# Turning q and probabilities with VectorE and a trip through DRAM, in the steady part of a fused attention and feed-forward kernel on one core

## The chip, the cores and the metric

The kernel runs on one core of a Trainium2 chip. The metric is the device time of one execution in microseconds. The core's engines run their own instruction streams: TensorE (PE) multiplies matrices, VectorE (DVE) and ScalarE (ACT) work on elements, GpSimd (POOL) does next to nothing here, and SyncE (SP) issues all transfers of the steady part in the order of its stream. Engines wait for each other and for transfers through semaphores.

## The reference

Attention over 8 batches, 8 heads, 576 tokens, 64 dimensions, with keys and values averaged in groups of eight tokens (72 pooled ones), followed by a feed-forward network with a softplus:

```
k_p = k.reshape(B, H, 72, 8, D).mean(axis=3);  v_p likewise
scores = (q @ k_p.T) / sqrt(D)
attn = exp(scores - max(scores));  attn /= sum(attn) + 1e-09
x = (attn @ v_p) as [4608 tokens, 512]
out = softplus(x @ w_in[512, 2048]) @ w_out[2048, 512]
```

All is float32. In this kernel the feed-forward products run as three products of rounded parts (a high and a low part of each factor).

## The kernel before, in words

The 4608 tokens are cut into 18 chunks of 256 (`CT`), each of two tiles of 128 tokens (`T`). The program has a first part, which splits the weights into high and low parts and works off chunks 0 to 2 with an order of its own, and a **steady part**, from chunk 3 on (`N1`), which the change is about. It begins at about 168 us of the span.

In the steady part a chunk's feed-forward work is eight **pairs** of weight blocks, u = 0 to 7. A pair has *first products* (`pair1`, 24 matmuls of 128x256 into a bank `h`, L727) and *second products* (from chunk 4, `NF`, on: `pair2_fast`, 21 matmuls into the banks `m`, L879, a scheme of seven products in place of eight). Between them stand ScalarE's two softplus passes (`g` L735, `gh` L749), VectorE's `gl` (L756), four additions `sf` (L789 to L792), and the split of the sums into `so` (ScalarE L803, VectorE L808). The first products of pair u are followed by the second products of pair u-1, so that these have a pair's time. The first-layer weights of a pair, two blocks of 512 KB, are streamed from DRAM by `load_wi` (L907) into one of two places; their issue waits for the first products two pairs ahead.

While chunk c is in its feed-forward part, the attention of chunk c+1 is done between its pairs (`steady_attention` and `probabilities`):

- q is loaded (`load_q_tile` L363, 128 tokens x 8 heads x 64), turned by eight 128x128 transposes on TensorE into two banks `qTp` (`Tile.qT`, L394), and copied out by ScalarE (`qT_out`, L401);
- the scores are made (`pair_scores`, L541), VectorE takes off the least and writes `E` (L563, L579), ScalarE makes the exponentials in place (L355, with a change of its function table);
- VectorE, once per tile, sums (L445), adds 1e-9 and inverts (L449, L450), multiplies into `pm` (keys 0 to 63, L454) and `pe` (keys 64 to 71, L589), and turns `pm` in blocks of 32x32 into `turn` (`turn`, L512). Four transfers within the core (`spread`, L518, 128 KB each) then bring the blocks to the partitions where they belong, in `pT`;
- the attention products (`av_products`, L641 and L648, tile `avp`) read `pT` and the pooled values and give the next chunk's `x` (L655, L658).

The order is written by a planner, the class `Order`: a list scheduler. Each piece of work (`op`) has an engine, a cost, what it comes after, the buffers it needs and a lag; its rank is the length of the chain behind it plus a number `first`, and the engines' streams are written in the order of the planned starts. Nothing of the plan is decided on the chip: each engine, SP's queue among them, works its own stream in order and waits where it must.

In both kernels the buffers are named by kinds with a few places each (`ld`, `G`, `qT`, `bank` and others); the pooled keys and values, which come through `ld`, are made in `keys_values`. Turned blocks are read back by `blocks` (L521).

```
before = first_products(c, u, before)
if u == EXP and c + 1 < NCH:
    rest(third[c, u])          # exponentials after this pair's sums
if u: before = second_products(c, u - 1, before)
```

Of the kernel before, what the change touches and what calls it, by code (L numbers as in the profile page):

```python
# [108 lines left out]
def pooled_attention_softplus_ffn(  # L109
# [14 lines left out]
    P = 128  # L124
# [381 lines left out]
    B32 = 32  # L506
    turned_ = set()
    A = P // B32
# [12 lines left out]
    def blocks(x, t):  # L521

        return x.rearrange("p a (i u m) -> p u m (a i)", u=T, m=HP)[:, t]
# [402 lines left out]
    def act(n):  # L926
        return 0.14 + 0.00094 * n
# [338 lines left out]

    def keys_values(b, free_k=None, free_v=None):
# [9 lines left out]
        def pooled(load, pool, time, slot, after=()):  # L1277

            s = Slot("ld")
            o = op(SYNC, time, lambda: load(s), ends[-2:][:1], [s], lag=2.4)  # L1280
            ends.append(op(DVE, 1.4, pool, [o, *after], [s, slot]))
            return ends[-1]

        sums_ = [pooled(lambda s, i=i: x["k_load"](i, s), lambda i=i: x["k_pool"](i), 1.2, s_kp)
                 for i in range(HP)]
        s_t = Slot("bank")
        o = op(PE, 0.3, lambda: k_transposes(bank(s_t, "kT"), x["kp"][0]), [*sums_, *free_k],
               [s_t, s_kp], first=100, home=None if todo.last else "h")
        k_ready[b] = [op(ACT, act(288), lambda: k_scaled(b, s_t.tile), [o], [s_t])]
        sums_ = [pooled(lambda s, i=i: x["v_load"](i, s), lambda i=i: x["v_pool"](i), 1.2, s_vp)  # L1290
                 for i in range(2)]
        v_ready[b] = [op(ACT, act(256), lambda: v_scaled(b, x["vp"][0]), [*sums_, *free_v], [s_vp])]
        o = pooled(lambda s: x["left_load"](s), x["left"], 1.0, s_vl, v_ready[b])
        o = op(DVE, 1.1, x["lasts"], [o, *k_ready[b]], [s_vl, s_lt])
        parts = [op(ACT, 0.65, lambda i=i: left_part(b, i, x["st"]["lt"]), [o, *free_v], [s_lt])
                 for i in range(2)]
        v_ready[b].append(op(DVE, 0.7, lambda: left_part(b, 2, x["st"]["lt"]), parts, [s_lt]))

    def combinations(u, free=None):
# [6 lines left out]
        for part in range(2):  # L1306
# [5 lines left out]
            if s:  # L1312
                o = op(SYNC, 2.0, lambda part=part: put_t(u, part), [o], s, lag=2.4,
                       first=0 if todo.last else 1000)
# [54 lines left out]
    op = todo.op  # L1369
    EXP, third = 2, {}  # L1370
    HURRY, EARLY = 60, 100
    MM = 0.1142
    TURN, SPREAD = 0.75, 3.0
# [6 lines left out]

    def steady_attention(c):
# [5 lines left out]
        o_q = op(SYNC, 3.0, load, qT_done.get(c - 1, ()), [s_q], lag=2.4)  # L1387
# [3 lines left out]
        s_qT, s_qb = [Slot("qT") for _ in tiles], [Slot("bank") for _ in tiles]  # L1391

        def transposes():
            for x, s in zip(tiles, s_qb):
                x.qT(bank(s, "qTp"))
        o = op(PE, 0.89, transposes, [o_q, *av_done.get(c - 1, ())], [s_q, *s_qb], first=EARLY, home="m")
        qT_done[c].append(o)
        for x, s, n in zip(tiles, s_qb, s_qT):
            x_q.append(op(ACT, act(512), lambda x=x, s=s, n=n: x.qT_out(s.tile, n.name), [o], [s, n]))
# [5 lines left out]
        p = op(PE, 1.4, lambda: pair_scores(  # L1405
# [3 lines left out]
        for j in (2, 0, 1):  # L1409
            ps = lambda j=j: third_bank() if j == 2 else ss[j].tile  # L1410
            o = op(DVE, 0.3 if j == 2 else 0.68,
                   lambda j=j, ps=ps: pair_least(c, j, ps(), s_mn.name), [p], [ss[j], s_mn],
                   first=HURRY if j == 2 else 0)
            for part in range(1 if j == 2 else 3):
                subs.append(op(DVE, 0.3 if j == 2 else (0.46, 0.3, 0.22)[part],
# [4 lines left out]
    def probabilities(c, tiles, s_E, s_lt, subs, where):  # L1420

        s_pT, lows, s_pe, es = Slot("pT"), [], Slot("pe"), []
        turns, turned, s_t = {}, [], Slot("ld")
        ex = op(ACT, 1.2 + TABLE, lambda: exponential(e_[c]), [*subs, where], [s_E])
        op(ACT, TABLE, lambda: None, [ex], first=5000)
        for x in tiles:
            s_sm, s_pm = Slot("sm"), Slot("G")
            o = op(DVE, 0.76, lambda x=x, n=s_sm: x.sum(n.name), [ex], [s_E, s_sm])
            o = op(DVE, 0.38, x.reciprocal, [o], [s_sm])
            m = op(DVE, 0.7, lambda x=x, s=s_pm: x.main(s.name), [o], [s_E, s_sm, s_pm])  # L1430
# [207 lines left out]
```

## Time and profile before

| | us |
|---|---|
| median of three runs | 871.7 (870.2, 871.7, 875.04) |
| the profiled execution | 874.31 |
| its span | 872.6 |
| mean granted TensorE clock | 0.999 |
| TensorE busy | 861.0, 8642 instructions |
| VectorE busy | 669.8, 1629 instructions |
| ScalarE busy | 405.3, 824 instructions |
| HBM read and written | 167.25 and 22.54 MB, 218 GB/s over the span |

The span is the time from the first to the last instruction on the core that the profile shows; the execution's own time is 1.7 us more. Busy time leaves out waiting. A matmul's record runs until its result is out and matmuls overlap, so the start of the next row tells what a group costs, not the sum of its records.

### The profile page before, as it was taken

The page shows a single profiled execution, that of the slowest core. Times are in us where ns is not written, and L with a number is a line of the kernel's source. Part 1 is how long each engine was busy: PE and PEld are TensorE (multiplying, and loading weights), DVE is VectorE, ACT ScalarE, POOL GpSimd, SP SyncE. Part 2 cuts the span into 40 slices and gives each one's busy share as a digit, 9 for nine tenths or more (in the row PEclk, how much of TensorE's full clock was granted, in tenths as well). Part 3 has the DMA queues.
Part 4 walks back from the last instruction along what each step waited for, and adds up shares of the span by engine and source line. Part 5 has one row for each costly group of instructions (what it writes and reads, how often), then busy time and mean ns, then how long its engine had stood idle before and what let it go on. Part 6 is the DMA issues. An engine that isn't in the chain of part 4 may idle for free.

```text
span 872.6 us, 21294 instructions
## 1 busy us (share of the span) xinstructions
PE 861.0 (99%) x8642; PEld 836.9 (96%) x8642; DVE 669.8 (77%) x1629; ACT 405.3 (46%) x824; POOL 3.8 (0%) x33
## 2 busy tenths in 40 slices
PE   8999999999999999999999999999999999999997
PEld 6799999999999999999999999999999999999997
DVE  5899999888886878787878867787767575848554
ACT  5964443354454444444544435353545444444332
POOL 1000000000000000000000000000000000000000
PEclk9999999999999999999999999999999999999999
DMA  8965545544989789678769766769666657556562
GB/s 257 330 211 179 209 148 170 172 156 158 314 287 291 244 259 289 213 261 251 254 224 286 235 230 226 235 230 271 225 228 207 230 218 241 217 192 222 204 248 80
DMA packets 115154, 198.52 MB, mean 228 GB/s; under 512 B 46960, under 2 KB 68464, under 8 KB 115056
## 3 DMA queue, kind: packets, MB, share of 16 engines
q1 hardware_dynamic: 115056, 197.16, 69.1%
q8 instruction: 68, 1.11, 0.5%
q14 instruction: 30, 0.25, 0.1%
HBM read 167.25 MB, written 22.54 MB: 218 GB/s over the span
## 4 chain that ended last, share of the span: by engine, by line
PE 89%; DMA 5%; DVE 4%; ACT 1%; issue 0%; SPq 0%; DVEq 0%; ACTq 0%
PE h L727 34%; PE m L879 27%; PE acc L699 7%; PE h L674 7%; PE acc L770 3%; PE avp L641 2%; DMA l<-wi 2%; PE qTp L394 1%; PE avp L648 1%; DMA vst<-in_v_dram 1%; PE sc L541 1%; DMA kst<-in_k_dram 1%; DVE o L900 1%; DMA kvst<-in_k_dram 1%; PE kps L1118 1%; DMA pT<-turn 1%
## 5 line engine op out<-in xcount | busy, mean ns | idle before, releaser
L727 PE MATMUL h<-x,l 128*128 128x256 f32 x2748 | 336.2, 278 | 1.7 <-DMA l<-wi 1.7
L727 PEld LDWEIGHTS h<-x,l 128*128 128x128 f32 x2748 | 321.8, 188 | 3.4 <-PE m L879 2.0
L735 ACT ACTIVATE g<-h 128x512 f32<-128x512 f32 x120 | 71.8, 599 | 263.0 <-PE h L727 262.9
L879 PE MATMUL m<-w,so 128*128 128x256 f32 x1134 | 148.2, 277 | 0.1
L879 PEld LDWEIGHTS m<-w,so 128*128 128x128 f32 x1134 | 137.6, 188 | 0.6 <-DVE o L900 0.3
L789 DVE TENSOR_TENSOR sf<-g 128x128 f32<-128x128 f32 x112 | 32.4, 289 | 102.5 <-ACT g L735 102.3
L803 ACT CAST so<-sf 128x512 fp32r<-128x512 f32 x112 | 69.7, 622 | 82.2 <-DVE sf L792 81.0
L879 PE MATMUL m<-w,gh 128*128 128x256 f32 x476 | 90.4, 278 | 0.5 <-DVE E L579 0.4
L808 DVE TENSOR_TENSOR so<-sf,so 128x512 fp32r<-128x512 f32 x112 | 77.0, 687 | 15.0 <-ACT so L803 15.0
L879 PEld LDWEIGHTS m<-w,gh 128*128 128x128 f32 x476 | 71.8, 188 | 0.9 <-issue 0.9
L756 DVE TENSOR_TENSOR gl<-g,gh 128x384 fp32r<-128x384 f32 (+1 forms) x120 | 67.3, 561 | 2.6 <-ACT gh L749 2.6
L879 PE MATMUL m<-w,gl 128*128 128x256 f32 x238 | 65.9, 277 | 0.0
L749 ACT ACTIVATE gh<-h 128x384 fp32r<-128x384 f32 (+1 forms) x120 | 59.4, 495 | 0.0
L679 ACT ACTIVATE g<-h 128x256 fp32r<-128x256 f32 x96 | 32.1, 382 | 55.4 <-PE h L674 32.7
L674 PE MATMUL h<-x,w 128*128 128x256 f32 x396 | 49.7, 278 | 0.2 <-ACT g L679 0.2
L674 PEld LDWEIGHTS h<-x,w 128*128 128x128 f32 x396 | 47.0, 188 | 0.6 <-ACT g L679 0.4
L699 PE MATMUL acc<-w,g 128*128 128x256 f32 x264 | 46.9, 278 | 0.0
L879 PEld LDWEIGHTS m<-w,gl 128*128 128x128 f32 x238 | 44.7, 188 | 0.0
L900 DVE TENSOR_TENSOR o<-o,m 128x256 f32<-128x256 f32 x98 | 39.7, 418 | 3.7 <-PE m L879 0.5
L699 PEld LDWEIGHTS acc<-w,g 128*128 128x128 f32 x264 | 39.7, 188 | 0.1
L699 PE MATMUL acc<-w,gl 128*128 128x256 f32 x132 | 36.6, 277 | 0.5 <-DVE gl L685 0.5
L879 PE MATMUL m<-l,gh 128*128 128x256 f32 x196 | 36.9, 277 | 0.0
(217 smaller groups left out, 1313.5 us busy)
## 6 DMA issues: line engine op xcount, KB each, us to landing
l<-wi SPq DMA_DIRECT2D x224, 512.0 KB
out_dram<-o SPq DMA_DIRECT2D x36, 256.0 KB
q<-in_q_dram SPq DMA_DIRECT2D x32, 256.0 KB
pT<-turn SPq DMA_DIRECT2D x56, 128.0 KB
kst<-in_k_dram SPq DMA_DIRECT2D x24, 288.0 KB
vst<-in_v_dram SPq DMA_DIRECT2D x24, 256.0 KB
stage<-in_moe_w_in_dram SPq DMA_DIRECT2D x22, 256.0 KB
stage<-in_moe_w_out_dram SPq DMA_DIRECT2D x11, 512.0 KB
```

Source lines behind the costliest of these rows:

```text
L674: nc.tensor.matmul(out=ps[:, 0:CT], lhsT=row(w, kc), rhs=x[:, kc], start=first and kc == j == 0, stop=last and kc == KC - 1 and j == 2)
L679: nc.scalar.activation(out=g, in_=ps[:, 0:CT], func=AF.Softplus)
L699: nc.tensor.matmul(out=accs[c][t][:, ns], lhsT=a[:, ts], rhs=w[:, ns], start=f == 0 and n == j == 0, stop=f == FC - 1 and n == 1 and j == ...
L727: nc.tensor.matmul(out=ps[:, k * CT:(k + 1) * CT], lhsT=row(w, kc), rhs=x_[c][i][:, kc], start=first and n == 0, stop=last and n == len(or ...
L735: nc.scalar.activation(out=g, in_=x.rearrange("p (b i) -> p b i", i=P), func=AF.Softplus)
L749: nc.scalar.activation(out=gh, in_=quarters(c, x.rearrange("p (b i) -> p b i", i=P)), func=AF.Softplus)
L756: nc.vector.tensor_tensor(out=gl, in0=quarters(c, g), in1=gh.bitcast(F32), op=ALU.subtract)
L789: tt(out=sf[:, 2], in0=g[:, 0], in1=g[:, 2], op=ALU.add)
L803: nc.scalar.copy(out=so[:, 0], in_=ss[c, u])
L808: nc.vector.tensor_tensor(out=so[:, 1], in0=sf, in1=so[:, 0].bitcast(F32), op=ALU.subtract)
L879: nc.tensor.matmul(out=ms[c][n], lhsT=x, rhs=y, start=u == 0 and j == 0 and n in (1, 6, 5, 4), stop=u == FP - 1 and j == 2 and n in (2, 7, ...
L900: nc.vector.tensor_tensor(out=o, in0=in0, in1=m[n], op=how)
```

## The change

In chunks 5 to 17 q is no longer turned by TensorE. VectorE turns it in blocks of 32x32 in one instruction of 128x1024, four transfers (`leave`, 128 KB each) write the blocks to a DRAM buffer `moved_q`, and one transfer (`enter`, 512 KB) reads it back with the blocks on their partitions. ScalarE copies the two tiles out of it with a stride. The probabilities of these chunks go the same way, through `moved_p`; the sum, the reciprocal, the two products and the turn are now one instruction each for both tiles, and the transfers inside the core are gone. Chunk 4's q is turned by TensorE as before, and its probabilities too (`BY_PE`): two times four transposes into `ptp`, copied by ScalarE. The buffer `pm` moves from kind `G` to kind `ld`; the turned q takes an `ld` buffer.

The planner of the steady part gets other costs, most of them a few per cent apart; a transfer is now an issue on SP and a piece of work on one shared `TRANSFER` resource, with a lag of 1.75 us (`LANDING`). The first part's costs stay. One wait is added: the second products of chunk 4's first pair come after the scores of chunk 5. At the end a table `SOONER` adds numbers to the `first` of some 200 pieces of work.

```diff
-    def turn(x, t, half, how):
-        nc.vector.transpose(
-            out=x.rearrange(how, s=A, u=T, m=HP)[:, t],
-            in_=half.rearrange("p (m r c s) -> p m s r c", m=HP, r=2, s=A))
-    def spread(x, o, a):
-        nc.sync.dma_start(out=o[:, a],
-                          in_=x[a * B32:(a + 1) * B32].rearrange("p (s x) -> p s x", s=A))
+    BY_PE = (4,)
+    moved = {x: dram.tile([A, B32, A, T * HP * B32], F32, name=f"moved_{x}") for x in "pq"}
+    def turn(x, half):
+        n = half.shape[1] // P
+        nc.vector.transpose(out=x.rearrange("p s (m i) -> p m s i", i=B32), in_=half)
+    def leave(x, to, a):
+        nc.sync.dma_start(out=moved[to][:, :, a].rearrange("s d x -> d s x"), in_=x[a * B32:(a + 1) * B32])
+    def enter(o, to):
+        nc.sync.dma_start(out=o.rearrange("p a x -> p (a x)"), in_=moved[to].rearrange("s d a x -> (s d) (a x)"))
...
+    TRANSFER, LANDING, nothing = "transfer", 1.75, lambda: None
+    LAGS = {PE: 0.2, ACT: 0.05, DVE: 0.05, TRANSFER: LANDING}
+    def op(engine, cost, fn, after=(), slots=(), lag=None, **more):
+        if engine is not SYNC:
+            return todo.op(engine, cost, fn, after, slots, LAGS[engine], **more)
+        queue, work = cost
+        o = todo.op(SYNC, queue, fn, after, slots, 0, **more)
+        return todo.op(TRANSFER, work, nothing, [o], slots, LANDING, first=more.get("first", 0))
...
+            o = op(DVE, 1.28, turn_q, [o_q], [s_q, s_t])
+            ways = [op(SYNC, (0.55, 0.4), lambda a=a: leave(turns["q"], "q", a), [o, *entered["q"]], [s_t], lag=2.3) for a in range(A)]
+            entered["q"] = [op(SYNC, (0.35, 1.3), enter_q, ways, [s_q], lag=3.2)]
+            for x, n in zip(tiles, s_qT):
+                x_q.append(op(ACT, act(512), lambda x=x, n=n: gather_q(x, n), entered["q"], [s_q, n]))
...
+            o = op(DVE, 1.4, sums_p, [ex], [s_E, s_sm])
+            o = op(DVE, 0.44, reciprocals, [o], [s_sm])
+            m = op(DVE, 1.27, main_p, [o], [s_E, s_sm, s_pm], first=FIRST)
+            es.append(op(DVE, 0.33, ends_p, [o], [s_E, s_sm, s_pe]))
+            o = op(DVE, 1.28, turn_p, [m], [s_pm, s_t], first=FIRST)
+            ways = [op(SYNC, (0.55, 0.4), lambda a=a: leave(x["turn"], "p", a), [o, *entered["p"]], [s_t], lag=2.3, first=FIRST) for a in range(A)]
+            entered["p"] = [op(SYNC, (0.35, 1.3), enter_p, ways, [s_pT], lag=3.2, first=FIRST)]
+            lows.extend(entered["p"])
...
-            o = op(SYNC, 3.3, lambda: load_wi(c, u), [p1[i]], lag=2.2, first=9)
+            o = op(SYNC, (0.75, 2.8), lambda: load_wi(c, u), [p1[i]], lag=2.2, first=9)
...
+            wait += score_done[c + 1] if (c, u) == (NF, 0) else []
...
+    SOONER = {4: 600.0, 18: 300.0, 35: 300.0, 48: -150.0, 50: 800.0, 53: -150.0, 57: -500.0, 58: -300.0, 62:
...
+    for i, x in SOONER.items():
+        todo.ops[i].first += x
```

TensorE, at the last place where q was turned (chunk 17's q, between chunk 16's pairs; `h` are first products, `m` second products, `qTp` the turned q), before and after:

```order
L879 MATMUL m<-l,so 128x256 x6
L879 MATMUL m<-l,gh 128x256 x2
L879 MATMUL m<-l,gl 128x256
L394 MATMUL qTp<-ident,q 128x128 x8
L727 MATMUL h<-x,l 128x256 x24
```

```order
L882 MATMUL m<-l,so 128x256 x6
L882 MATMUL m<-l,gh 128x256 x2
L882 MATMUL m<-l,gl 128x256
L730 MATMUL h<-x,l 128x256 x24
L882 MATMUL m<-w,gh 128x256 x2
```

The eight transposes are gone and the first products follow the second products directly. Over the whole order the score products of a chunk now stand one chunk earlier, and the exponentials of a chunk one pair earlier; the attention products stay behind the first products of pair 7.

SP, the issues around the end of chunk 15's and the beginning of chunk 16's feed-forward part (`wi_130` and up are weight blocks; two make a pair), before and after:

```order
L907 DMA l<-wi_142 128x1024
L907 DMA l<-wi_143 128x1024
L518 DMA pT<-turn 128x1x256 x4
L907 DMA l<-wi_144 128x1024
L907 DMA l<-wi_145 128x1024
L907 DMA l<-wi_130 128x1024
L907 DMA l<-wi_131 128x1024
L907 DMA l<-wi_132 128x1024
L907 DMA l<-wi_133 128x1024
L363 DMA q<-in_q_dram 128x8x64 x2
```

```order
L910 DMA l<-wi_142 128x1024
L910 DMA l<-wi_143 128x1024
L519 DMA moved_p<-turn 32x4x256 x4
L910 DMA l<-wi_144 128x1024
L910 DMA l<-wi_145 128x1024
L522 DMA pT<-moved_p 128x1024
L910 DMA l<-wi_130 128x1024
L910 DMA l<-wi_131 128x1024
L519 DMA moved_q<-turn 32x4x256 x4
L910 DMA l<-wi_132 128x1024
L910 DMA l<-wi_133 128x1024
L522 DMA qT<-moved_q 128x1024
```

The four transfers of p stand where they stood and now lead to DRAM; one pair's weights later the transfer back is queued, ahead of the next pair's weights. q's way out and back follows in the same manner; its load now stands before these rows.

VectorE, the last chunk's probabilities (`sm` the sums and their reciprocals, `pm` and `pe` the products, the others the feed-forward part), before from the second tile's addition on, and after from the row behind the reciprocal's pair on:

```order
L449 TENSOR_SCALAR sm<-sm 128x8
L450 RECIPROCAL sm<-sm 128x8
L512 STREAM_TRANSPOSE turn<-pm 128x4x4x32
L789 TENSOR_TENSOR sf<-g 128x128
L790 TENSOR_TENSOR sf<-g 128x128
L791 TENSOR_TENSOR sf<-sf,g 128x128
L792 TENSOR_TENSOR sf<-g,sf 128x128
L756 TENSOR_TENSOR gl<-g,gh 128x384
L454 TENSOR_TENSOR pm<-E,sm 128x512
L808 TENSOR_TENSOR so<-sf,so 128x512
L512 STREAM_TRANSPOSE turn<-pm 128x4x4x32
L589 TENSOR_TENSOR pe<-E,sm 128x64 x2
```

```order
L1487 TENSOR_REDUCE sm<-E 128x16
L1491 TENSOR_SCALAR sm<-sm 128x16
L1492 RECIPROCAL sm<-sm 128x16
L792 TENSOR_TENSOR sf<-g 128x128
L793 TENSOR_TENSOR sf<-g 128x128
L794 TENSOR_TENSOR sf<-sf,g 128x128
L795 TENSOR_TENSOR sf<-g,sf 128x128
L759 TENSOR_TENSOR gl<-g,gh 128x384
L811 TENSOR_TENSOR so<-sf,so 128x512
L1495 TENSOR_TENSOR pm<-E,sm 128x1024
L792 TENSOR_TENSOR sf<-g 128x128
L793 TENSOR_TENSOR sf<-g 128x128
L794 TENSOR_TENSOR sf<-sf,g 128x128
L795 TENSOR_TENSOR sf<-g,sf 128x128
L515 STREAM_TRANSPOSE turn<-pm 128x8x4x32
```

Sum, product and turn stand once for both tiles, with one pair's feed-forward rows between reciprocal and product, and four more additions between product and turn.

## Rows read from the trace of the kernel before

**Rows 1.** The page's first lines: the span, and busy time, share and instructions of each engine.

```profile
span 872.6 us, 21294 instructions
PE 861.0 (99%) x8642; PEld 836.9 (96%) x8642; DVE 669.8 (77%) x1629; ACT 405.3 (46%) x824; POOL 3.8 (0%) x33
```

**Rows 2.** The chain of work that ended last, its share of the span by engine.

```profile
PE 89%; DMA 5%; DVE 4%; ACT 1%; issue 0%; SPq 0%; DVEq 0%; ACTq 0%
```

**Rows 3.** What TensorE waited for, whole span: engine, line of the waiting instructions, what released them; us in total, times, longest us.

```profile
PE h L727 <- DMA l<-wi: 1.7, 2, 0.8
...
PE avp L641 <- DMA pT<-turn: 0.4, 1, 0.4
```

**Rows 4.** TensorE's timeline in chunk 11's stretch and the next: start us, duration us, line, operation, tiles, shapes, count.

```profile
592.10 2.88 PE L727 MATMUL h<-x,l 128*128 128x256 f32 x24
594.82 0.39 PE L879 MATMUL m<-l,gh 128*128 128x256 f32 x2
...
597.21 1.04 PE L394 MATMUL qTp<-ident,q 128*128 128x128 f32 x8
598.00 2.98 PE L727 MATMUL h<-x,l 128*128 128x256 f32 x24
600.81 0.39 PE L879 MATMUL m<-l,gh 128*128 128x256 f32 x2
...
633.50 1.10 PE L641 MATMUL avp<-pT,vs 64*64 64x128 f32 x32
```

**Rows 5.** TensorE's timeline in the first part, where it turns probabilities.

```profile
67.76 0.60 PE L475 MATMUL ptp<-ident,pm 128*128 128x128 f32 x4
68.11 0.48 PE L699 MATMUL acc<-w,g 128*128 128x256 f32 x2
...
68.55 0.39 PE L699 MATMUL acc<-w,g 128*128 128x256 f32 x2
...
68.89 0.39 PE L699 MATMUL acc<-w,g 128*128 128x256 f32 x2
```

**Rows 6.** VectorE's groups by line and shape, whole span: busy us, mean ns of one; idle time before them.

```profile
L512 DVE STREAM_TRANSPOSE turn<-pm 128x512 f32<-128x512 f32 x28 | 29.9, 1071 | 0.0
L454 DVE TENSOR_TENSOR pm<-E,sm 128x512 f32<-128x512 f32 x36 | 24.7, 686 | 0.8
...
L445 DVE TENSOR_REDUCE sm<-E 128x8 f32<-128x576 f32 x30 | 21.2, 747 | 14.6 <-ACT E L355 14.6
...
L563 DVE TENSOR_REDUCE mn<-sc 128x7 f32<-128x504 f32 x28 | 18.5, 674 | 0.0
...
L1016 DVE TENSOR_TENSOR w<-stage,w 128x1024 fp32r<-128x1024 f32 x11 | 13.2, 1219 | 0.2 <-ACT w L1012 0.2
...
L450 DVE RECIPROCAL sm<-sm 128x8 f32<-128x8 f32 x36 | 7.3, 203 | 1.2
...
L449 DVE TENSOR_SCALAR sm<-sm 128x8 f32<-128x8 f32 x36 | 5.9, 163 | 1.4 <-ACT E L439 1.3
...
L589 DVE TENSOR_TENSOR pe<-E,sm 128x64 f32<-128x64 f32 x28 | 4.5, 204 | 0.0
...
L563 DVE TENSOR_REDUCE mn<-m 128x2 f32<-128x144 f32 x12 | 3.6, 303 | 0.2 <-PE m L541 0.2
```

**Rows 7.** Stretches of the span, all but the last line those of one chunk's feed-forward part (the first has nine pairs, the others shown eight); the last line is the time of one group of p's transfers. Columns: from and to, length, busy us and instructions of PE, PEld, DVE, ACT and POOL, granted clock, share of time in which the core's 16 DMA engines were busy, GB/s.

```profile
235.50:286.50 51.00, 50.90 (x508) 49.88 (x505) 39.35 (x105) 22.33 (x40) 0.11 (x1) 1.00 0.92 289
...
418.60:466.30 47.70, 46.75 (x460) 45.25 (x458) 38.18 (x104) 22.56 (x41) 0.10 (x1) 1.00 0.73 232
466.30:513.30 47.00, 46.16 (x461) 44.97 (x455) 34.71 (x93) 20.41 (x36) 0.10 (x1) 1.00 0.82 263
...
559.40:604.50 45.10, 45.10 (x461) 44.23 (x455) 36.81 (x98) 20.31 (x36) 0.10 (x1) 1.00 0.83 252
...
741.40:786.60 45.20, 45.20 (x456) 44.47 (x454) 30.13 (x82) 20.32 (x36) 0.10 (x1) 1.00 0.60 211
443.70:447.40 3.70, 3.70 (x35) 3.70 (x34) 3.15 (x13) 2.86 (x6) 0.00 (x0) 1.00 0.32 72
```

**Rows 8.** ScalarE's group of copies of the turned q, columns as in rows 6.

```profile
L401 ACT COPY qT<-qTp 128x512 f32<-128x512 f32 x36 | 19.7, 590 | 9.1 <-PE qTp L394 8.9
```

**Rows 9.** SP's timeline: four transfers of turned probabilities, from the first issue's start to the last one's end.

```profile
582.12 2.51 SPq L518 DMA_DIRECT2D pT<-turn  x4
```

**Rows 10.** VectorE's timeline from the exponentials to the second turn, in the stretch of rows 4: start, duration, line, operation, in brackets the idle time before and what ended it.

```profile
617.58 1.41 DVE L445 TENSOR_REDUCE sm<-E 128x8 f32<-128x576 f32 x2 [1.79 <-ACT E L355]
...
619.49 0.29 DVE L789 TENSOR_TENSOR sf<-g 128x128 f32<-128x128 f32 x1 [0.19 <-ACT g L735]
...
620.43 0.55 DVE L756 TENSOR_TENSOR gl<-g,gh 128x384 fp32r<-128x384 f32 x1
620.90 0.68 DVE L454 TENSOR_TENSOR pm<-E,sm 128x512 f32<-128x512 f32 x1
621.50 0.68 DVE L808 TENSOR_TENSOR so<-sf,so 128x512 fp32r<-128x512 f32 x1
...
626.41 1.09 DVE L512 STREAM_TRANSPOSE turn<-pm 128x512 f32<-128x512 f32 x1
```

**Rows 11.** The chain that ended last in order of time, two of its transfers: start us, duration us.

```profile
352.43 4.43 DMA pT<-turn
...
469.66 7.85 DMA l<-wi
```

More of the change, by code (lines that the diff above doesn't have):

```diff
@@ L1265, in feed, with either @@
                 s.users.append(todo.last)
+    def either(first, steady):
+        return first if todo.last else steady
     def keys_values(b, free_k=None, free_v=None):
@@ L1312, in combinations @@
             if s:
[L1313 removed]
+                o = op(SYNC, either(2.0, (0.4, 1.4)), lambda part=part: put_t(u, part), [o], s, lag=2.4,
                        first=0 if todo.last else 1000)
@@ L1422, in probabilities @@
         s_pT, lows, s_pe, es = Slot("pT"), [], Slot("pe"), []
-        turns, turned, s_t = {}, [], Slot("ld")
-        ex = op(ACT, 1.2 + TABLE, lambda: exponential(e_[c]), [*subs, where], [s_E])
+        ex = op(ACT, 1.21 + TABLE, lambda: exponential(e_[c]), [*subs, where], [s_E])
         op(ACT, TABLE, lambda: None, [ex], first=5000)
[L1426 to L1430, printed above, removed]
-            es.append(op(DVE, 0.23, lambda x=x, s=s_pe: pair_ends(c, x, s.name), [o], [s_E, s_sm, s_pe]))
-            def turn_p(x=x):
-                if x.t == 0:
-                    turns["p"] = one.tile([P, T * H * KM], F32, tag=s_t.name, name="turn")
-                turn(turns["p"], x.t, x.pm.rearrange("p h j -> p (h j)"), "p (s u m i) -> p u m s i")
-            turned.append(op(DVE, TURN, turn_p, [m, *turned], [s_pm, s_t]))
@@ L1441, in spread_p @@
                 pt_[c] = one.tile([P, A, T * HP * B32], F32, tag="Z", name="pT")
                 turned_.add(c)
-            spread(turns["p"], pt_[c], a)
-        for a in range(A):
-            lows.append(op(SYNC, 0.4, lambda a=a: spread_p(a), turned, [s_t, s_pT], lag=SPREAD, first=EARLY))
+                enter(pt_[c], "p")
+            o = op(DVE, 1.4, sums_p, [ex], [s_E, s_sm])
+            o = op(DVE, 0.44, reciprocals, [o], [s_sm])
+            m = op(DVE, 1.27, main_p, [o], [s_E, s_sm, s_pm], first=FIRST)
@@ L1507, in load_sums @@
         t_ready.setdefault(u, []).append(
-            op(SYNC, 2.0, lambda: load_t(u, part), [*after, made[u, part] if u >= U1 else None],
+            op(SYNC, (0.42 * (part + 1), 1.4), lambda: load_t(u, part), [*after, made[u, part] if u >= U1 else None],
                lag=2.4))
@@ L1551, in output @@
             s_u = Slot("G")
-            o = op(ACT, 0.4, lambda: finish(c, 0, [s.name for s in (*s_o, s_u)]), ends[:1],
+            o = op(ACT, 0.41, lambda: finish(c, 0, [s.name for s in (*s_o, s_u)]), ends[:1],
                    [*s_o, s_u, banks[0]], first=HURRY)
-            i = op(DVE, 1.27, lambda: finish(c, 1), [o], [*s_o, s_u, *banks[:2]], first=HURRY)
-            o = op(DVE, 1.7, lambda: finish(c, 2), [i, ends[1]], [*s_o, s_u, *banks[2:]],
+            i = op(DVE, 1.36, lambda: finish(c, 1), [o], [*s_o, s_u, *banks[:2]], first=HURRY)
+            o = op(DVE, 1.81, lambda: finish(c, 2), [i, ends[1]], [*s_o, s_u, *banks[2:]],
                    first=HURRY)
@@ L1568, in output @@
             i = T - 1 - t if len(ends) > 1 else t
-            op(SYNC, 1.0, lambda t=t, i=i: put(c, i, out_[c][t]), [copies[t]], [s_o[t]], lag=2.2,
+            op(SYNC, (0.35, 0.75), lambda t=t, i=i: put(c, i, out_[c][t]), [copies[t]], [s_o[t]], lag=2.2,
                first=2000)
```

108 lines of the change are left out of this document (79 added, 29 removed), and 31 rows, old and new, of the table SOONER.

## The prediction, made before the changed kernel was run

> **What bounds the kernel now.** I read the page from its first part down. Busy time comes first [rows 1]: TensorE works 861.0 us of a span of 872.6, VectorE 77% of it, ScalarE 46%. One engine has no room and the others do. The chain that ended last says the same from the other side [rows 2]: 89% of it is TensorE, 5% transfers, 4% VectorE. TensorE's waits are the third view [rows 3]: in the whole steady part the first products waited for streamed weights twice, 1.7 us together, and the attention products once for the turned probabilities, 0.4 us. So a TensorE instruction that goes away shortens the run by its own time, as long as nothing that replaces it arrives late; and whatever is added on VectorE, ScalarE or the queues costs nothing until it is late. The profiled execution took 874.31 us, 1.7 more than its span and 2.6 more than the median of the three runs (871.7). The sum is made against 874.3, and 2.6 is taken off at the end.
>
> **q leaves TensorE.** In a steady chunk the eight transposes of q stand between second products and the next first products [rows 4]: they start at 597.21 and the first products after them at 598.00, so 0.79 us. The first products behind them then take 598.00 to 600.81, 2.81 us, against 2.72 (592.10 to 594.82) behind second products; I count that 0.09 too, as the price of the switch. 0.88 us a chunk, 13 chunks (5 to 17): **-11.44 us**. The order shows nothing put in their place on TensorE.
>
> **Chunk 4's p goes to TensorE.** The nearest row is the first part, which turns its probabilities so [rows 5]: four transposes 67.76 to 68.11, 0.35 us, and the next three matmuls 0.44 us (68.11 to 68.55) against 0.34 (68.55 to 68.89). 0.45 for each of two tiles: **+0.90 us**. Net -10.54. The wait that the change adds, for chunk 5's scores ahead of chunk 4's first second products, ties two pieces of TensorE's own queue; by the new order the scores stand ahead of them anyway, so it holds nothing up. If it did, chunk 5's q would be late once: its transfers, priced as p's below, are 6.3 + 7.85 us at the most and they stand on SP ahead of the first streamed weights. I count nothing.
>
> **VectorE.** Today a chunk's probabilities cost, twice, sum 747 ns, addition 163, reciprocal 203, product 686, transpose 1071, ends 204 [rows 6]: 6.15 us. After, each is done once at double width. Sum: 747 ns plus 576 elements at 1.03 ns, the slope between 303 ns for 144 and 674 for 504, 1.34 us; product 1.22, which is what a 128x1024 TENSOR_TENSOR took; ends 0.27; addition and reciprocal about 0.37. The transpose is the unknown: no row has a 128x1024 one. It cannot cost less than today's 1.07, and two of today's are 2.14; I take 2.14, since the row gives no hint of a fixed part. Together 5.34, and q's transpose 2.14: +1.3 us a chunk, -0.8 at the other end. VectorE is busy 30 to 39 us in stretches of 45 to 51 [rows 7], so this is hidden; were it not, 13 x 1.3 = 17 us would show.
>
> **ScalarE and the SP queue.** ScalarE makes two 128x512 copies for q as before, of 590 ns [rows 8], from another place and with a stride; at twice that it would add 1.2 us to an engine idle for half the time. Nothing. SP issues six more transfers per chunk (four that leave and one that enters for q, one that enters for p). Four issues took 2.51 us [rows 9], so +3.8 at most; SP only issues, and what matters is what stands behind. By the new order p's four leave after one weight pair's issues, the entering one stands after the next pair's, and a third pair's blocks stand behind it, held until the four have landed. Pairs are issued 5.11 us apart; if the four start as late as that, the last lands 1.9 + 4.43 us on (both below) and the third pair's issue, due after another 5.11, is 1.2 us late: a part of the 7.5 us that it has (below). Nothing in the sum; it speaks for rival 2.
>
> **The path of p is the one that can be late.** Today [rows 10] the exponentials are done when the sum starts, 617.58, and the second transpose ends at 627.50: 9.92 us, since VectorE does two pairs' work of the feed-forward part in between. The products that need p start at 633.50 [rows 4], 15.92 after 617.58. After the change the exponentials come one pair earlier, while the products keep their place behind the last first products; a pair is 5.11 us (592.10 to 597.21), so 21.0 us are there. What must fit: sum, reciprocal, product, transpose 1.34 + 0.37 + 1.22 + 2.14 = 5.07; ahead of the transpose, by the new order, one pair's rows, 1.41 and 0.68 (619.49 to 620.90, and the row at 621.50), and four more additions, 0.94 (619.49 to 620.43): 8.1 us. Then the transfers to memory: four issues, the last starting 1.9 us (three quarters of 2.51) after the first, landing in 4.43 us, the hop of 128 KB that the chain shows [rows 11]: 6.3. Then the one that brings 512 KB back, which starts only when all four have landed: at the least the same 4.43, at the most the 7.85 that a 512 KB weight block took when it was late [rows 11]. Sum 18.8 to 22.2 against 21.0: 2.2 us to spare, or 1.2 late. I take it as in time, because 7.85 comes from one of only two waits in 14 x 8 pairs, and the middle, 20.5, still fits.
> The row gives 4.43 us for 128 KB within the core. The Trainium skill (DMA: Bandwidth & Descriptors, "Anatomy of one DMA — SWDGE (gpsimd) path") puts a transfer at some 2.0 us fixed plus bytes at 436 GB/s, and says that most of the fixed part is the receipt of the write, heaviest where memory outside the core is the target. By its figures, an estimate, a leaving transfer takes 2.3 us and the entering one 3.2, the path 15.4, and the late case is gone; by its remark on the target the hop is longer than one inside the core, which speaks for the late case. The row is about twice the page's figure, so the measurement decides, and the sum keeps its own ends. q has no such question: by the new order its transfers are issued a chunk ahead of its scores.
>
> **Transfers.** A weight pair is asked for when the first products two pairs ahead end, and it must land within two second products and one first: 2.39 + 2.72 + 2.39 = 7.5 us [rows 4]. Added per chunk are 0.52 MB that leave for q and two times 0.52 MB that enter. At 252 GB/s the engines were busy to .83 [rows 7], so 304 GB/s full; while one of p's hops ran, 72 GB/s at .32, so 225 full. 0.52/225 + 1.05/304 = 2.33 + 3.45 = 5.8 us, .13 of a stretch of 45.2. Most stretches stand at .60 to .83 and have the room. The first, at .92, has 51 x .08 = 4.1 us left and is 1.7 over.
>
> **The sum.** 874.3 - 11.44 + 0.90 = 863.8 for an execution like the profiled one; less 2.6, **861.2 us**.
>
> **Rivals.**
> (1) *The planner's corrections also take away the old delays.* Two stretches took 47.7 and 47.0 us where an equal one took 45.2 [rows 7], 2.5 + 1.8 = 4.3 us, at landings of streamed data that the new list issues at other places. For it: one of the two holds the 7.85 us landing [rows 11], and SP's issues around such places stand in another order now. Against it: the same transfers plus 5.8 us per chunk. 861.2 - 4.3 = 857.
> (2) *Streamed weights come late.* In the six stretches at .80 and over (from 235.50 to the last at 559.40) [rows 7] the added 5.8 us push a pair past its 7.5. The price is what such a delay cost: 2.15 on average (2.5 and 1.8), five times, and 1.7 in the first: 12.4, so 861.2 + 12.4 = 874, the whole gain back; half of it gives 867. For it: SP puts p's hops between the pairs, and 7.85 was seen. Against it: the stretch at .83 lost nothing (45.1 us).
> (3) *p is late: slower.* With the long end of its path the attention products of all 13 chunks wait 1.2 us, 15.6 in all: 861.2 + 15.6 = 877. It decides from 10.54/13 = 0.81 us per chunk. For it: two hops, one after the other, in place of one, the first fully landed before the second starts. Against it: one wait of 0.4 us in 14 chunks now, and a whole pair more of time.
> (4) *It does not do what it says*: the transposes go, but other work that was hidden behind them comes to light at once, as first products that wait 0.8 us for g or weights. About 872. Against it: [rows 3] leave next to nothing that waits.
>
> **Chances.** Half a per cent, 4.4 us, is about what a measurement of this kernel can tell from no change: faster means under 867.3, slower over 876.1. Forecast .69; rival 1 .11; rival 2 .12, of it .03 on the faster side; rival 3 .06; rival 4 .02. Faster .69 + .11 + .03 = .83, same .11, slower .06. The range: down to 855.5, which is rival 1 less the 1.5 us by which the fastest of the three runs is below the median; up to 870, which is the forecast with rival 2 at over half or a p path 0.7 late. Left out are rivals 3, 4 and the dear end of 2.
>
> **What would show it.** In the profile after: TensorE 10 to 11 us less busy, and no q transposes but chunk 4's; first products follow second products directly. VectorE busy 10 to 20 us more, if a double transpose costs two. Waits of the attention products for pT of at most a few tenths; of first products for weights near 1.7 us in all. Wrong would be: an attention product that waits over 0.5 us in most chunks (rival 3), streamed weights as TensorE's first wait with over 6 us (rival 2), or stretches near 45.2 us without q's transposes (rival 4); they should be near 44.3.

## The result, and the profile after

The changed kernel is **slower**: 880.3 us, the median of 14 runs (873.2 to 887.0), against 872.9 of the kernel before (14 runs, 870.2 to 875.7), ratio 1.0082, 95% interval 1.0054 to 1.0110 (the ratios in this document leave out runs more than 1.5% above the fastest of their kernel, here the one of 887.0). The forecast was 861.2, its range 855.5 to 870.0. The profiled execution took 875.09, span 873.4; a second one, 880.73, is shown further down.

The page's first part, to be laid beside [rows 1]:

```profile
span 873.4 us, 21152 instructions
PE 855.2 (98%) x8546; PEld 829.9 (95%) x8546; DVE 669.3 (77%) x1562; ACT 405.9 (46%) x826; POOL 3.8 (0%) x33
```

TensorE has 96 instructions fewer (104 transposes gone, 8 come), but is busy only 5.8 us less and the span is longer. Where? TensorE's waits, beside [rows 3]:

```profile
PE avp L644 <- DMA pT<-moved_p: 2.8, 1, 2.8
PE avp L644 <- DVE sf L793: 1.9, 1, 1.9
PE warm L347 <- DVE ones L342: 1.5, 1, 1.5
PE m L882 <- DVE gl L759: 1.4, 1, 1.4
PE acc L773 <- DVE gl L759: 1.0, 1, 1.0
PE m L882 <- ACT so L806: 0.8, 1, 0.8
```

The attention products waited twice: for p's trip at 276 us, and at 327, put down to a VectorE row that has nothing to do with them (where p's trip is shortened and the order kept, in half_wi4 below, this wait is gone, and in another execution of this kernel, further down, it is put down to the trip). Stretches by chunk and three short windows show what follows; columns as in [rows 7]:

```profile
229.70:276.50 46.80, 42.23 (x390) 41.36 (x390) 38.95 (x89) 22.89 (x42) 0.00 (x0) 1.00 0.92 313
276.50:327.70 51.20, 48.16 (x510) 46.38 (x511) 39.13 (x100) 22.59 (x41) 0.21 (x2) 0.97 0.84 272
327.70:375.60 47.90, 47.88 (x482) 47.48 (x482) 35.16 (x89) 19.81 (x35) 0.10 (x1) 0.93 0.90 292
...
509.00:553.20 44.20, 44.20 (x448) 43.34 (x447) 34.06 (x87) 20.28 (x36) 0.10 (x1) 1.00 0.96 292
...
275.00:280.00 5.00, 3.54 (x23) 2.77 (x24) 2.48 (x9) 1.30 (x3) 0.00 (x0) 0.66 0.99 355
325.00:330.00 5.00, 3.07 (x56) 2.78 (x56) 3.60 (x8) 1.62 (x4) 0.00 (x0) 0.78 0.94 315
330.00:335.00 5.00, 5.00 (x26) 5.00 (x27) 2.88 (x6) 1.69 (x3) 0.00 (x0) 0.53 1.03 307
```

Read the clock column. A chunk without such waits now takes 44.2 us where an equal one took 45.2 [rows 7]: the gain per chunk is there, even at a DMA share of .96. But behind each late landing TensorE, having stood idle for 2 to 3 us, goes on at about half speed, the lower of its two levels: 0.66 in 275 to 280, 0.78 and 0.53 in 325 to 335. In 330 to 335 an engine busy all the time got through 26 matmuls, where 24 take 2.72 us otherwise [rows 4]. From the start of the attention products to the next first products TensorE took 5.78 us in the first place (276.46 to 282.24) and 7.74 in the second (327.71 to 335.45); in half_wi4, at full clock, the same instructions took 4.11 and 4.65. So the waits of 2.8 and 1.9 us cost some 4.5 and 5.0. Over 240 to 340 us, the kernel before first, after second:

```profile
240.00:340.00 100.00, 99.48 (x1021) 97.89 (x1020) 79.61 (x213) 46.74 (x82) 0.21 (x2) 1.00 0.87 270
```

```profile
240.00:340.00 100.00, 92.61 (x909) 90.16 (x908) 74.57 (x183) 43.96 (x79) 0.21 (x2) 0.95 0.90 295
```

7 us more idle, 4.7 of them the two waits for p, and 5% of the clock, about 5 us: more than the whole gain, in these 100 us.

p's trip of chunk 5 stands in SP's timeline (first fence) and in the chain in order of time (second); the third has the exponentials, the fourth VectorE's sum and the row of the probabilities behind it:

```profile
262.57 0.92 SPq L910 DMA_DIRECT2D l<-wi  x2
263.95 2.04 SPq L519 DMA_DIRECT2D moved_p<-turn  x4
267.47 1.02 SPq L363 DMA_DIRECT2D q<-in_q_dram  x2
268.54 3.00 SPq L300 DMA_DIRECT2D vst<-in_v_dram  x2
271.70 0.47 SPq L522 DMA_DIRECT2D pT<-moved_p  x1
```

```profile
258.31 7.97 DMA qT<-moved_q
...
266.30 1.15 ACT qT L1440 x2
...
271.70 4.63 DMA pT<-moved_p
276.33 0.14 issue
276.46 2.09 PE avp L644 x16
```

```profile
252.45 1.17 ACT L355 ACTIVATE E<-E 128x1152 f32<-128x1152 f32 x1
```

```profile
253.98 1.34 DVE L1487 TENSOR_REDUCE sm<-E 128x16 f32<-128x1152 f32 x1
...
260.93 0.17 DVE L1491 TENSOR_SCALAR sm<-sm 128x16 f32<-128x16 f32 x1
```

From the first leaving issue to the landing in `pT` are 12.4 us (263.95 to 276.33). The forecast had 6.3 + 4.43 to 7.85, so 10.7 to 14.2: the trip as a whole kept inside it. The way back itself landed in 4.63 us, near its cheap end. But it was issued 7.75 us behind the first leaving issue, although the four issues took only 2.04. SP works its issues in order, and two things stood ahead of the way back: the load of q, which waited until ScalarE had copied out what q's own trip brought back (7.97 us from its issue at 258.31 to the landing, the copies done at 267.45), and two loads of v, whose issues took 3.00 us. What came on top lies ahead of the trip: the exponentials were done at 253.62 (252.45 and 1.17) and the first leaving transfer was issued at 263.95, 10.3 us where the forecast had 8.1. Between the sum and the next row of the probabilities stood the feed-forward rows of two pairs.

Chunk 6, SP's timeline:

```profile
313.24 1.14 SPq L519 DMA_DIRECT2D moved_p<-turn  x2
...
316.84 1.31 SPq L363 DMA_DIRECT2D q<-in_q_dram  x2
318.19 4.65 SPq L288 DMA_DIRECT2D kst<-in_k_dram  x1
323.26 0.34 SPq L522 DMA_DIRECT2D pT<-moved_p  x1
```

Here 10.0 us lie between the first leaving issue and the way back, with weights, a load of q and loads of k in between; the last of k alone took 4.65 us to issue. No row gives the landing; with the 4.63 us of chunk 5 it would be at 327.9, an estimate, and the products started at 327.71. In chunks 7 to 17 only the next weights stand between the two, it is 3.8 to 6.8 us, and no attention product waited.

The other engines did as forecast or better: VectorE's busy time is unchanged (669.3 us against 669.8), since the double transpose took 1.24 us, where the forecast had 2.14:

```profile
L515 DVE STREAM_TRANSPOSE turn<-pm 128x1024 f32<-128x1024 f32 x13 | 16.1, 1240 | 0.2
```

### The profile page after: what moved, and what is told of

Read it like the earlier page. It is cut to its first block, busy times and chain, and to the rows that moved or that the text cites. A ratio compares the mean times of both kernels' runs of the same rounds, so it can differ in the third digit from the quotient of the medians.

```text
span 873.4 us, 21152 instructions
## 1 busy us (share of the span) xinstructions
PE 855.2 (98%) x8546; PEld 829.9 (95%) x8546; DVE 669.3 (77%) x1562; ACT 405.9 (46%) x826; POOL 3.8 (0%) x33
## 4 chain that ended last, share of the span: by engine, by line
PE 89%; DVE 4%; DMA 4%; ACT 1%; SPq 1%; issue 0%; DVEq 0%; ACTq 0%
PE h L730 34%; PE m L882 29%; PE h L677 7%; PE acc L702 7%; PE avp L644 2%; PE acc L773 2%; PE avp L651 2%; PE sc L544 1%; DMA qT<-moved_q 1%; DMA t<-t 1%; DMA kvst<-in_k_dram 1%; PE kps L1121 1%; DMA l<-wi 1%; DMA pT<-moved_p 1%; DMA out_dram<-o 1%
```

## The experiments

Theory A: the trips are late where transfers are dense (chunks 4 to 6); TensorE waits, and its clock falls. Rival B: the new list, with its corrections, is the worse order. Rival C: p's hop has no slack under any list, and density alone decides. Medians, each against runs of the kernel before on the same chip (their medians 871.9 to 873.4):

| run | us | ratio (95%) |
|---|---|---|
| half_wi | 872.9 | 1.0010 (0.9986, 1.0034) |
| half_wi4 | 865.0 | 0.9898 (0.9847, 0.9950) |
| before_half_wi | 871.7 | 0.9980 (0.9963, 0.9997) |
| no_trips | 867.4 | 0.9948 (0.9927, 0.9969) |
| no_enter_p | 870.3 | 0.9991 (0.9968, 1.0014) |
| hop_same | 873.4 | 1.0032 (1.0004, 1.0061) |
| early_p | 914.5 | 1.0470 (1.0442, 1.0498) |
| hop | 920.5 | 1.0536 (1.0509, 1.0563) |
| all_pe | 917.5 | 1.0507 (1.0472, 1.0543) |
| no_corrections | 899.8 | 1.0327 (1.0296, 1.0358) |
| old_list_q | 890.0 | 1.0212 (1.0175, 1.0249) |
| old_list_q8 | 871.5 | 0.9992 (0.9971, 1.0012) |
| q8_p_sooner | 871.5 | 0.9984 (0.9959, 1.0010) |
| q8_half_wi | 865.5 | 0.9895 (0.9855, 0.9935) |
| old_list_q8_hop | 905.6 | 1.0388 (1.0360, 1.0416) |
| q8_pool | 924.8 | 1.0574 (1.0538, 1.0610) |
| changed_pool_p | 901.9 | 1.0324 (1.0285, 1.0364) |

**Halved weights, every instruction in its place.** In `load_wi`, from chunk 5 (half_wi) or 4 (half_wi4) on:

```diff
-            nc.sync.dma_start(out=w.bitcast(F32), in_=wi_dram[f])
+            nc.sync.dma_start(out=w[:, 0].bitcast(F32), in_=wi_dram[f][:, 0])
```

half_wi: 

> The changed kernel with the same instructions in the same order on every engine; from chunk 5 on each streamed weight block is 256 KB in place of 512 (only its high half is loaded, so the feed-forward results of these chunks are not the reference's). Theory A (transfers are too dense in chunks 4 to 7, so the round trip of the probabilities through DRAM lands after TensorE has come to the attention products, TensorE waits 2 to 3 us, and its granted clock falls behind each wait): the trip from exponentials to landing shrinks from 22 us to 16 or 17 in chunks 5 and 6, the waits at 276 and 327 us go with the clock dips behind them, 862 to 868 us. Rival B (the new list with its corrected priorities puts work on VectorE and ScalarE in a worse order, the transfers have nothing to do with it): same order, so 876 to 882 us.

half_wi4: 

> The changed kernel in the same order, with the streamed weight blocks 256 KB in place of 512 from chunk 4 on (the first half_wi began at chunk 5, after the late trip at 276 us; the low halves of the weights are stale in these chunks). Theory A: the trip of chunk 5's probabilities, 23 us, shrinks below 20, the wait at 276 us and the clock dip go, and what stays is what the new list loses without any trip: 867 to 869 us, as no_trips. If the wait at 276 stays, the length of the trip does not come from the streamed weights: 872.

half_wi gave back 7.4 us, less than A asked for: the trip at 276 us runs during chunk 4, whose weights it had left whole, and its wait stayed (3.5 us). From chunk 4 on, the time is 865.0, 15 us below the changed kernel. Its windows, for the same chunks as above, and its waits (those of the avp and gl groups):

```profile
230.00:273.00 43.00, 41.99 (x393) 41.38 (x391) 38.03 (x85) 22.73 (x42) 0.00 (x0) 1.00 0.83 259
273.00:320.50 47.50, 46.33 (x510) 44.94 (x510) 38.55 (x100) 22.11 (x41) 0.21 (x2) 1.00 0.69 207
320.50:365.90 45.40, 45.36 (x485) 44.98 (x485) 36.98 (x93) 20.56 (x37) 0.10 (x1) 1.00 0.70 204
```

```profile
PE acc L773 <- DVE gl L759: 0.9, 1, 0.9
...
PE avp L644 <- DMA pT<-moved_p: 0.8, 1, 0.8
```

The same three chunks take 43.0 + 47.5 + 45.4 = 135.9 us against 145.9, at a clock of 1.00; the whole profiled execution took 864.2 against 875.1. With the order kept, only the transfers are less dense. What that shortened is the stay on SP. Chunk 5, from SP's timeline:

```profile
262.46 1.83 SPq L519 DMA_DIRECT2D moved_p<-turn  x4
...
266.27 1.64 SPq L300 DMA_DIRECT2D vst<-in_v_dram  x2
268.07 0.47 SPq L522 DMA_DIRECT2D pT<-moved_p  x1
```

The way back was issued 5.6 us behind the first leaving issue, where it was 7.75 (in chunk 6 7.5, where it was 10.0), and v's loads took 1.64 us to issue in place of 3.00. The way back's own landing was not faster, 4.78 us against 4.63. So the density works through the order on SP. A high share alone makes no chunk late: at .96 (509.00 to 553.20 above) no attention product waited. Whether the way back put ahead of those loads would have been enough, with whole weights, no run tells. The control:

> The kernel before with the streamed weight blocks halved from chunk 4 on, nothing else: the control for the two runs with halved weights. If the density of transfers matters only to what the change adds, 870 to 872 us. If the kernel before is held up by it too, it wins back its waits for weights and for pT, at most the 4.3 us of its two long stretches: 867 to 869.

871.7: the kernel before hardly gains (ratio 0.998), so what the dense transfers hold up is what the change adds. Beside it half_wi4 shows the change with 6.7 of the 10.5 us that the forecast had for it.

**Trips taken away, the order kept.** In no_trips `leave` and `enter` are empty for q and p; in no_enter_p only p's way back; in hop_same p's four transfers go within the core (`hop_p`) and `enter` is empty:

```diff
-                enter(pt_[c], "p")
+                pt_[c] = pt_[4]
...
+            def hop_p(a):
+                nc.sync.dma_start(out=pt_[c][:, a], in_=x["turn"][a * B32:(a + 1) * B32])
```

no_trips: 

> The changed kernel with every piece of work in the same order on every engine, but no transfer to or from DRAM for q and for the probabilities of chunks 5 to 17: ScalarE copies q out of its loaded tile, the attention products read chunk 4's probabilities (so from chunk 5 on the attention is not the reference's). Theory A (the trips, late in the early chunks, are what takes the gain back): no avp wait, no clock dip, 861 to 865 us, which is what the prediction's sum gives. Rival B (the new list's order costs it): 874 us or more, the waits for gl and so at 189, 252 and 310 us stay, as do losses behind them.

no_enter_p: 

> The changed kernel in the same order with only the transfer back of the probabilities left out: they still leave for DRAM, and the attention products read chunk 4's probabilities, so nothing waits for the trip (from chunk 5 on the attention is not the reference's). Theory A: 863 to 867 us, the waits at 276 and 327 us gone. Rival B: 876 to 882. Rival C (density): 870 or more, with waits elsewhere for transfers.

hop_same: 

> The changed kernel with the same pieces of work in the same order, but the four transfers of the probabilities go within the core to where they belong, as before the change, and the transfer back from DRAM is left out; q goes through DRAM. Theory A: the path from exponentials to landing is 4.5 us shorter, so the attention products wait in no chunk for over 0.5 us, 863 to 868 us, with less spread than the changed kernel's 14. Rival B: 876 to 882. Rival C (the density of transfers, q's trip above all, and not p's second trip): 873 to 878.

p's way back alone is worth 880.3 - 870.3 = 10.0 us, all trips 12.9; a single hop gives back 6.9 of the 10. None reaches the forecast's 861: without any trip 867.4 stay, where the kernel before less the forecast's 10.5 is 862.4. So B holds for 5 us at the most; half_wi4, which has the new list and all trips, took 2.4 us less, so a part of them hangs on the transfers too. no_trips' waits:

```profile
PE h L730 <- DMA l<-wi: 1.6, 1, 1.6
...
PE m L882 <- DVE gl L759: 1.3, 1, 1.3
PE m L882 <- ACT so L806: 1.1, 2, 0.8
PE acc L773 <- DVE gl L759: 1.0, 1, 1.0
```

The first is one late landing of weights behind 500 us. The others, 3.4 us, stand before 310 us, at the same places as in the changed kernel. Behind one of them stands this row of ScalarE's timeline, a buffer still being written out as the combined weights `t`:

```profile
247.87 0.62 ACT L806 CAST so<-sf 128x512 fp32r<-128x512 f32 x1 [4.66 <-DMA t<-t]
```

That these waits are the list's whole part is read, not tested.

**Lists planned anew.** early_p turns the probabilities of chunks 5 to 7 by TensorE, hop has p's hop within the core, all_pe turns everything by TensorE (`BY_PE` split for q and p), no_corrections empties the table:

```diff
-    BY_PE = (4,)
+    Q_BY_PE, P_BY_PE = (4,), (4, 5, 6, 7)
...
-    for i, x in SOONER.items():
+    for i, x in ():
```

early_p: 

> The changed kernel with the probabilities of chunks 5, 6 and 7 turned by TensorE, as chunk 4's, at 0.9 us each, 2.7 us of TensorE work; q goes through DRAM as in the changed kernel. The table of corrections is applied to the same pieces of work. Theory A: the waits of the attention products of chunks 5 and 6 (3.1 and 2.2 us) and the clock dips behind them (about 4 us) go, 880.3 - 9.5 + 2.7 = 871 to 875 us; the granted clock is back at 0.997 or more. Rival B: nothing is won and 2.7 us are added, 883 us.

hop: 

> The changed kernel with the probabilities of chunks 5 to 17 brought to their partitions by four transfers within the core, as before the change, in place of four to DRAM and one back; q goes through DRAM, the turn stays one instruction of 128x1024 (its input read with a stride). Theory A: the second transfer of 4 to 5 us is gone from the path, the attention products wait nowhere for over 0.5 us, 861 to 867 us. Rival B: 878 to 882 us, since the list is still the new one. Rival C (q's trip through DRAM alone fills the transfers so that everything is late): 875 us or more.

all_pe: 

> The new list with q and probabilities of all steady chunks turned by TensorE, so without any trip through DRAM; TensorE does 13 x 0.88 + 13 x 0.90 = 23 us more than in the changed kernel. Theory A: the list costs nothing by itself, so the time is that of the kernel before plus the probabilities' transposes, 872.9 + 14 x 0.9 = 885 us, less what waits the hops still cost there, 882 to 887. Rival B: the changed kernel's own delays stay, 880.3 + 23 = 903, at least 893 us.

no_corrections: 

> The changed kernel with the table of corrections empty; q and probabilities take the same trips. The three kernels whose list was planned anew after an edit took 914 to 920 us, with TensorE waiting for VectorE. If the corrections are what makes the new list run at all, 900 to 925 us. If the re-planned lists suffered only because corrections found for one plan were applied to another, 875 to 885 us.

The first three came out 30 to 54 us above what Theory A had for them, and tell nothing of the trips: TensorE waits for VectorE (early_p: 12.0 us, longest 9.7, for `E`). no_corrections came out at the edge of what was expected (899.8, for 900 to 925); its first wait is again p's trip, 9.1 us in two chunks. hop and hop_same move the same data the same way and are 47 us apart; only the order differs. The corrections are worth 20 us in the one plan they were found for (899.8 without); three plans next to it took 914 to 921 us with them.

**One part alone, under the old list.** The kernel before, with q of chunks 5 (old_list_q) or 8 (old_list_q8) to 17 taken through DRAM; _hop takes it within the core:

```diff
+            o = op(DVE, 1.25, turn_q, [o_q], [s_q, s_t])
+            ways = [op(SYNC, 0.5, lambda a=a: leave_q(a), [o, *entered], [s_t], lag=5.0) for a in range(A)]
+            entered[:] = [op(SYNC, 0.4, enter_q, ways, [s_q], lag=5.0)]
```

old_list_q: 

> The kernel before with one part of the change alone: q of chunks 5 to 17 turned by VectorE and taken through DRAM, planned with the costs of the kernel before, without corrections; the probabilities go as before, by one hop within the core. Its removed TensorE work is 13 x 0.88 = 11.4 us. Theory A' (p's second trip and the new list cost it in chunks 3 to 6, q's trip is nearly free): 861 to 866 us. Rival C (any further trip in the dense early chunks is late): 867 to 874, with waits there.

old_list_q8: 

> As the run before, but q of chunks 4 to 7 is turned by TensorE and only that of chunks 8 to 17 goes through DRAM; up to chunk 7 the order is that of the kernel before. 10 x 0.88 = 8.8 us less work. Theory A': 863 to 866 us, the early stretches as in the kernel before, the later ones 0.9 to 1.0 us shorter each. Rival C: here nothing new lies in the dense chunks, so also 863 to 866; if it is slower than 867, neither the early chunks nor p's trip are the cause.

old_list_q8_hop: 

> As the run before, with q of chunks 8 to 17 moved by four transfers within the core in place of the trip through DRAM (the turn reads its input with a stride, about 2.1 us on VectorE). The path of q is shorter and VectorE's work longer; its scores come a chunk before they are needed either way. Both theories: 863 to 866 us; if TensorE waits for VectorE, more.

old_list_q and the hop variant came out far above what was expected, with waits for VectorE's `lt` (4.0 and 7.7 us, against 0.5 in old_list_q8), and say little. old_list_q8 is the telling one: up to chunk 7 the order is the same, ten chunks lose their transposes, and the time does not move. Over 867 us, its expectation said, would clear the early chunks and p's trip; what it shows is another late landing of p, with one hop. Its first wait:

```profile
PE avp L641 <- DMA pT<-turn: 4.3, 5, 2.3
```

Against 0.4, once, before [rows 3]. Around the longest, from 490 to 505 us, the clock was 0.91, 0.50 and 0.90 in steps of 5 us, some 3.4 us lost. The waits and this make 7.7 us, most of the 8.8 saved: p's path was next in line, and what TensorE saves, it waits in the main for p's one hop. Two runs bear on this, the first moving p's second product and turn sooner on VectorE, the second halving the weights:

q8_p_sooner: 

> The run with q of chunks 8 to 17 through DRAM under the old list, with one thing moved in these chunks: on VectorE the second tile's product stands right behind its reciprocal (ahead of the four additions and gl) and its turn right behind gl, so that both are some 1.2 us sooner; TensorE's, ScalarE's and SP's orders are the same word for word. Theory D (taking 0.88 us a chunk from TensorE brings the attention products to p's hop, which had 1.3 us to spare, and p's lateness takes the gain back): the waits for pT<-turn fall from 4.3 us to under 1.5, 866 to 869 us in place of 871.5. If p's path is not what takes it back: 871 to 873, the product and turn only push the feed-forward rows.

q8_half_wi: 

> The run with q of chunks 8 to 17 through DRAM under the old list, with the streamed weight blocks halved from chunk 4 on. If p's hop is late because the transfers are dense: it lands in 4.6 to 5 us in all chunks, the waits for pT<-turn (4.3 us in five chunks) go, 864 to 867 us. If the hop is late for another reason: 870 to 872.

q8_p_sooner won nothing (871.5), against what was expected: although VectorE's rows stand sooner, the waits for p were 6.1 us in its profile, again in five chunks. The hops were issued 9.3 or 10.4 us behind the exponentials, against 9.8 or 11.1 without the move: less than the 1.2 us expected, but sooner, and p was no less late. That speaks against VectorE's part of the path. With halved weights the gain appears, 865.5 (before_half_wi: 871.7), and the waits for p fall:

```profile
PE avp L641 <- DMA pT<-turn: 0.8, 2, 0.6
```

So C has a part in it: under the old list, too, p's path has no slack where transfers are dense.

**A queue of its own.** p's transfers issued by GpSimd (`nc.gpsimd.dma_start`):

q8_pool: 

> The run with q of chunks 8 to 17 through DRAM under the old list, with p's four hops issued by GpSimd, so on a queue of their own, in place of SP's, where they stand behind the weight blocks. If p's hop is late because its packets stand behind 512 KB blocks in the same queue: it lands in under 5 us, the waits for pT go, 864 to 867 us with the whole of the computation, faster than both kernels. If the engines' bandwidth is the limit and not the place in the queue: 870 to 872, the hop as long as before.

changed_pool_p: 

> The changed kernel with p's five transfers issued by GpSimd on a queue of their own. Place in the queue: the trip of chunks 5 and 6 falls below 20 us, 867 to 870 us. Bandwidth, or a slower issue on GpSimd: 878 us or more.

Worse by 53 and 22 us. The page lists the median from issue to landing for this queue, q8_pool first:

```profile
pT<-turn POOLq DMA_DIRECT2D x56, 128.0 KB, 6.0
```

```profile
moved_p<-turn POOLq DMA_DIRECT2D x52, 128.0 KB, 4.7
pT<-moved_p POOLq DMA_DIRECT2D x13, 512.0 KB, 5.5
```

So the place in SP's queue alone is not it, or GpSimd's queue is slower by itself; these runs do not part the two.

**The changed kernel once more.** 

> The changed kernel itself, once more with a profile: its 14 runs lie between 873 and 887 us, and the profile at hand is one of the shortest. Theory A: in a run of 880 us or more the attention products of further chunks wait for pT, since p lands with only 2 to 4 us to spare from chunk 7 on, and the granted clock falls behind each wait; the mean clock is 0.99. Rival B: the extra time lies in waits for VectorE and ScalarE.

880.73 us. The same two chunks, now both put down to p's trip, 4.1 us in chunk 5 and 1.4 in chunk 6, and streamed weights late three times:

```profile
PE avp L645 <- DMA pT<-moved_p: 5.5, 2, 4.1
PE h L731 <- DMA l<-wi: 2.1, 3, 0.8
```

```profile
275.00:280.00 5.00, 0.90 (x9) 0.70 (x11) 3.79 (x9) 1.60 (x3) 0.00 (x0) 0.90 1.01 330
280.00:285.00 5.00, 5.00 (x32) 4.21 (x25) 2.12 (x4) 1.39 (x3) 0.00 (x0) 0.50 0.95 323
```

A wait of 4.1 us, then 5 us at half clock; behind the wait of 1.4 us it stayed at 1.00 (330 to 340). No further chunk waited for p, against A's expectation. What makes one execution's landing later than another's is open.

## Why the prediction was wrong

- *q leaves TensorE, -0.88 a chunk*: right. Stretches without the waits went from 45.2 to 44.2.
- *Chunk 4's p, VectorE, ScalarE*: right or harmless. The transpose was priced at 2.14 and took 1.24.
- *p's path, 18.8 to 22.2 us against 21.0, "I take it as in time"*: **this step failed**. In chunk 5 it took 22.7, from the exponentials' end at 253.62 to the landing at 276.33, and TensorE was there after 20.1 (276.46 less the wait of 2.78), not 21.0. Late by 2.8, then by 1.9 a chunk on, where the dear end had 1.2. The dear end's own reason, a way back of 7.85 us, did not come true: it took 4.63. Too short were the two terms ahead of it. VectorE, put at 8.1, took 10.3 in chunk 5 (7.7 in chunk 6); the time to the issue of the way back, put at 6.3, was 7.75 in chunk 5 and 10.0 in chunk 6. Both terms are those of the order at one place, the last chunk for VectorE, chunks 15 and 16 for SP, taken for all chunks. Late in the run they hold or are near: in chunk 17 VectorE took 8.1 (800.40 to 808.53), and only weights stand between the hops. In chunks 5 and 6 loads of q and of v or k stand there as well. The prediction itself had the stretch at .92 as "1.7 over" and did not carry this to p: rivals 2 and 3 were weighed apart, and came as one.
- *Rival 3's price, 1.2 us in all 13 chunks*: two chunks waited, not thirteen, and the price of one was off as well. The two waits took the clock with them and cost some 9.5 us, nearly the 11.4 that thirteen chunks were to save. All trips together cost 12.9 us (no_trips).
- *The new list at nothing*: wrong by 5 us at the most, as no_trips stays at 867.4. The forecast read the order for what was moved, and asked of no moved piece whether its buffer would be free; that this is the reason is not tested.
- *The two hops by the Trainium skill*: by "Anatomy of one DMA — SWDGE (gpsimd) path" in DMA: Bandwidth & Descriptors, 2.0 us plus bytes, they would take 1.9 + 2.3 + 3.2 = 7.4 us, an estimate. The trace has 12.4 in chunk 5, the way back alone 4.63; the section's fit is for one transfer issued by GpSimd, these are SP's among others, and the measurement decides.

## What to carry to other kernels

When work is taken off the bound engine, look for the path that was nearly late before: its slack, and not the work removed alone, bounds what can be won, and old_list_q8 shows a saving of 8.8 us that won nothing. Price a trip through memory chunk by chunk, with the rows and issues that stand ahead of it there, and not by one place in the order. A wait that takes the clock with it counts more than its length: 2.8 and 1.9 us cost some 4.5 and 5.0 here. A table of corrections found for one plan belongs to that plan: judge an edit by keeping the order and emptying single pieces.

## What had not been expected of the hardware

- After idling 1.9 and 4.1 us TensorE ran at about half clock (0.53 in 330 to 335 us of the first execution, 0.50 in 280 to 285 of the second).
- Issues held SP for long: two loads of v took 3.00 us to issue and one of k 4.65, against 1.64 and 2.43 with halved weights (half_wi4), and the way back of p stood behind them.
- A 32x32 block transpose of 128x1024 took 1.24 us where the input was contiguous; read with a stride (hop_same) it took 2.03, nearly two of the 128x512 ones [rows 6]:

```profile
L1510 DVE STREAM_TRANSPOSE turn<-pm 128x1024 f32<-128x1024 f32 x13 | 26.3, 2026 | 0.2
```

- Transfers issued by GpSimd landed no sooner: 6.0 us in the median for 128 KB within the core, where the one of SP's in [rows 11] took 4.43.
